# First expert layer of chunks 0 and 1 in seven block products, VectorE's work dealt out by a count for each stretch

## The chip, the core and the metric

One core of one Trainium2 chip runs the whole program. The metric is the device time of one execution in microseconds, the median over several runs.

## What is computed

Attention with a decay (batch 2, 8 heads, 576 positions, head size 64), then a layer of 8 experts whose gates are normalised over rows and columns eight times, then a feed-forward layer with the mish function. All 1152 tokens go through all 8 experts:

```python
x = attention(q, k, v, f)              # 1152 x 512
P = exp(x @ w_gate - max)              # 1152 x 8
for _ in range(8):
    P /= P.sum(1); P /= P.sum(0); P *= N / E
for e in range(8):
    h = maximum(x @ w1[e], 0)          # 512 x 1024: the first expert layer
    out += P[:, e:e+1] * (h @ w2[e])   # 1024 x 512: the second
g = mish(out @ w_in)                   # 512 x 2048
return g @ w_out                       # 2048 x 512
```

## The kernel before

The 1152 tokens are three chunks `c` of 384. An expert is two halves of 512 hidden columns, so there are 16 halves, and a half is four tiles `gg` of 128 columns. A step is one tile of one half for one chunk. Every operand of a matrix product is split into a high and a low part (`xh`, `xl`; `w1h`, `w1l`; `hh`, `hlo`), and a product is made of three: high with high, high with low, low with high.

A step has a first layer (`l1`, L659: 12 matmuls of 128 x 384 into one PSUM tile `ph`), then `relu_split` (L671: ScalarE writes `hh`, VectorE `hlo`), then the second layer of the step before (`l2`, L680: 9 matmuls of 128 x 512 into three accumulators `pa`). So each step's `relu_split` has the second layer of the step before it as cover. After the last tile of an expert VectorE adds the three accumulators, times a column of P, to `acc` (`evict`, L813): nine such additions per expert.

The order is written out by hand (`manual_schedule`): each engine runs its instructions in the order of the code. The attention part ends with half 0 of chunks 0 and 1 (`filler`, L477). Then 184 steps follow (the loop at L855): eight of chunk 2 for expert 0, four each of chunks 0 and 1 for half 1, then 24 for each further expert. Beside them run, handed out one or two to a step: the eight rounds of the normalisation (`sinkhorn`, L693; one round in each of the first steps), the weights' loads and splits (`queue_split`, L779; ScalarE makes the high part, VectorE the low part, GpSimd in its place for half 1), and the decoding of `w_in` and `w_out`, which come as 64-bit numbers (`decode`, L734, and `part`, L758: nine VectorE operations on 128 x 256, 64 times, on every second step). Four weight slots are used in turn. Then come 48 steps of the mish layer (L961). In the attention part, steps `s` below 24 issue `warm(2)`, two small matmuls whose result nobody reads (L590).

## Time and profile before

| | |
|---|---|
| median of 3 runs | 1157.53 us (1154.59 to 1161.88) |
| the profiled execution | 1154.56 us, of which 1152.8 us from the first to the last instruction |
| TensorE (PE) | busy 1137.0 us, 6336 matmuls |
| VectorE (DVE) | busy 726.2 us |
| ScalarE (ACT) | busy 395.7 us |
| GpSimd (POOL) | busy 93.3 us |
| granted TensorE clock | 0.999 of full speed |

The attention part takes the first 180 us, the expert steps run from 180 to 949 us, the mish layer from there to the end. Matmuls overlap, so their own duration is longer than the distance between their starts; that distance is what a matmul costs. A VectorE instruction also starts a little before the end of the one ahead. An idle time is written behind the instruction that ended it, with the instruction that was waited for.

### The profile page before, as it was taken

Reading aid. Unit: us, or ns where it says so; the run is one execution under the profiler, and the core shown is the slowest. Engines: PE = TensorE matmul, PEld = TensorE weight load, DVE = VectorE, ACT = ScalarE, POOL = GpSimd, SP = SyncE. Lnnn points to the kernel's source line nnn. Section 1 sums busy time; section 2 is a strip of 40 time slices with the busy share of each in tenths; the row PEclk is TensorE's granted clock in tenths of the full one; section 3 lists DMA queues with packets and bytes.
Section 4 is the critical chain, followed back from the end, with each engine's and each line's share of the span. In section 5 each row is a group of like instructions: output and inputs, shape, how many; then the busy total and the mean of one; then the engine's idle time right before and its main releaser. Section 6 shows DMA issues by size and latency. Waiting matters only on the chain.

```text
span 1152.8 us, 16871 instructions
## 1 busy us (share of the span) xinstructions
PE 1137.0 (99%) x6336; PEld 1016.4 (88%) x6336; DVE 726.2 (63%) x1755; ACT 395.7 (34%) x864; POOL 93.3 (8%) x127
## 2 busy tenths in 40 slices
PE   8999999999999999999999999999999999999998
PEld 7777778999999999999999999999999999999997
DVE  7966655786657665765675676543222229988887
ACT  6766643322212222221221222122111115555554
POOL 5735423000000000000000000000000000000000
PEclk9999999999999999999999999999999999999999
DMA  6524202343323322331433243221350061000000
GB/s 155 119 62 99 72 13 74 101 130 126 129 73 110 128 92 92 124 127 60 128 116 104 76 144 111 69 69 55 110 183 1 1 220 72 1 29 1 28 1 28
DMA packets 91074, 98.90 MB, mean 86 GB/s; under 512 B 35936, under 2 KB 56160, under 8 KB 90992
## 3 DMA queue, kind: packets, MB, share of 16 engines
q1 hardware_dynamic: 90992, 97.81, 27.5%
q8 instruction: 50, 0.82, 0.3%
q14 instruction: 32, 0.26, 0.1%
HBM read 74.39 MB, written 19.21 MB: 81 GB/s over the span
## 4 chain that ended last, share of the span: by engine, by line
PE 94%; DVE 3%; ACT 1%; issue 1%; POOL 0%; DMA 0%; DVEq 0%; ACTq 0%; POOLq 0%
PE ph L665 42%; PE pa L685 41%; PE x L444 2%; PE pt L420 2%; PE pa L513 1%; PE sp L368 1%; PE ph L494 1%; PE sp L369 1%; PE pt L322 1%; DVE p L381 1%; PE wt L353 1%; PE x L846 0%; DVE rs L399 0%; PE g L460 0%; PE g L465 0%
## 5 line engine op out<-in xcount | busy, mean ns | idle before, releaser
L665 PE MATMUL ph<-xh,w1h 128*128 128x384 f32 x928 | 312.2, 336 | 0.0
L665 PE MATMUL ph<-xh,w1l 128*128 128x384 f32 x928 | 311.8, 336 | 0.0
L665 PE MATMUL ph<-xl,w1h 128*128 128x384 f32 x928 | 311.3, 336 | 0.0
L675 DVE SCALAR_TENSOR_TENSOR hlo<-ph,hh 128x384 fp32r<-128x384 f32 x184 | 102.6, 557 | 304.1 <-ACT hh L674 299.4
L674 ACT ACTIVATE hh<-ph 128x384 fp32r<-128x384 f32 x184 | 90.5, 492 | 575.5 <-PE ph L665 568.3
L685 PE MATMUL pa<-w2h,hh 128*128 128x512 f32 x696 | 273.1, 392 | 0.6 <-ACT hh L940 0.6
L685 PE MATMUL pa<-w2l,hh 128*128 128x512 f32 x696 | 272.6, 392 | 0.0
L685 PE MATMUL pa<-w2h,hlo 128*128 128x512 f32 x696 | 271.7, 390 | 0.0
L665 PEld LDWEIGHTS ph<-xh,w1h 128*128 128x128 f32 x928 | 174.3, 188 | 9.0
L665 PEld LDWEIGHTS ph<-xl,w1h 128*128 128x128 f32 x928 | 174.3, 188 | 8.5
L665 PEld LDWEIGHTS ph<-xh,w1l 128*128 128x128 f32 x928 | 174.3, 188 | 0.0
L685 PEld LDWEIGHTS pa<-w2h,hlo 128*128 128x128 f32 x696 | 130.7, 188 | 28.9 <-DVE hlo L945 0.9
L685 PEld LDWEIGHTS pa<-w2h,hh 128*128 128x128 f32 x696 | 130.8, 188 | 21.2 <-ACT hh L940 1.6
L685 PEld LDWEIGHTS pa<-w2l,hh 128*128 128x128 f32 x696 | 130.8, 188 | 18.9
L391 ACT ACTIVATE p<-p,nmax 128x256 f32<-128x256 f32 (+6 forms) x80 | 48.4, 605 | 13.9 <-DVE nmax L381 11.6
L404 POOL TENSOR_SCALAR p<-p,rs 128x256 f32<-128x256 f32 (+6 forms) x80 | 46.1, 588 | 57.1 <-DVE rs L400 37.7
L827 DVE SCALAR_TENSOR_TENSOR acc<-pa,P,acc 128x512 f32<-128x512 f32 x69 | 47.4, 743 | 0.1
L924 ACT ACTIVATE acc<-acc,two 128x384 f32<-128x384 f32 x48 | 29.6, 617 | 48.6 <-DVE acc L923 48.6
L381 DVE CUSTOM_DVE_ANT_0 p<-sp,mask 128x256 f32<-128x256 f32 (+6 forms) x80 | 37.6, 471 | 6.5 <-PE sp L369 5.3
L94 DVE TENSOR_TENSOR w1l<-stg,w1h 128x512 fp32r<-128x512 f32 x56 | 38.6, 692 | 0.1
L94 DVE TENSOR_TENSOR w2l<-stg,w2h 128x512 fp32r<-128x512 f32 x56 | 38.6, 692 | 0.0
L368 PE MATMUL sp<-kt,qa 128*128 128x256 f32 (+6 forms) x96 | 34.8, 365 | 3.3 <-DVE nmax L381 2.4
(154 smaller groups left out, 1207.6 us busy)
## 6 DMA issues: line engine op xcount, KB each, us to landing
stg<-in_moe_w_dram SPq DMA_DIRECT2D x64, 512.0 KB
raw<-in_moe_w_in_dram SPq DMA_DIRECT2D x32, 256.0 KB
raw<-in_moe_w_out_dram SPq DMA_DIRECT2D x32, 256.0 KB
w_in_h<-db SPq DMA_DIRECT2D x32, 128.0 KB
w_in_l<-da SPq DMA_DIRECT2D x32, 128.0 KB
w_out_h<-db SPq DMA_DIRECT2D x32, 128.0 KB
w_out_l<-da SPq DMA_DIRECT2D x32, 128.0 KB
w1h<-w_in_h SPq DMA_DIRECT2D x4, 1024.0 KB
```

Source lines behind the costliest of these rows:

```text
L94: (lo_engine or nc.vector).tensor_tensor(out=lo, in0=raw, in1=f(hi), op=ALU.subtract)
L368: nc.tensor.matmul(out=t[:n, :w], lhsT=a1, rhs=kt[:, h, ks], start=True, stop=False)
L381: nc.vector.tensor_tensor_reduce(out=p[:n, a, o:o + w], in0=t[:n, :w], in1=mask[:n, m0 + o:m0 + o + w], scale=-1.0, scalar=prev, op0=ALU.a ...
L391: nc.scalar.activation(out=p[:n, a, :nk], in_=p[:n, a, :nk], func=AF.Exp, bias=prev, scale=-1.0, accum_out=u["ssum"][:n, a:a + 1],)
L404: nc.gpsimd.tensor_scalar(out=p[:n, a, :nk], in0=p[:n, a, :nk], scalar1=r[:n, a:a + 1], scalar2=1.0, op0=ALU.mult, op1=ALU.mult,)
L420: nc.tensor.transpose(out=pt[:, o + j * n:o + (j + 1) * n], in_=p[:n, a, j * 128:(j + 1) * 128], identity=idn[:n, :n],)
L665: nc.tensor.matmul(out=ph, lhsT=w[wn][:, kk, fs], rhs=x[c][:, kk], start=(kk == 0 and n == 0), stop=(kk == KD - 1 and n == 2),)
L674: nc.scalar.activation(out=hh, in_=ph, func=AF.Relu)
L675: nc.vector.scalar_tensor_tensor(out=hl, in0=ph, scalar=0.0, in1=f(hh), op0=ALU.max, op1=ALU.subtract)
L685: nc.tensor.matmul(out=pa[j], lhsT=a_[:, ts_], rhs=w[wn][:, ft_, :], start=(first and n == 0), stop=(last and n == 2),)
L827: nc.vector.scalar_tensor_tensor(out=acc[t], in0=pa, scalar=sc, in1=acc[t], op0=ALU.mult, op1=ALU.add)
L924: nc.scalar.activation(out=e_, in_=w_, func=AF.Ln, bias=two)
```

## The change

For halves 1 to 15, the first layer of chunks 0 and 1 is computed together (`pair`). The half's `w1` (512 x 512) and the two chunks (512 x 768) are cut into two by two blocks, and seven products of blocks take the place of eight: four use sums `s` of blocks of `w1`, made anew for each half (`s_sum`, `s_split`), four use sums `t` of blocks of the chunks, made once (`t_whole` on GpSimd, `t_diff` and `t_split`). Each product comes for two row tiles `g`, so a half has 14 products of six matmuls. What products share is kept by adding into the same PSUM bank, and by ScalarE copies of a bank (`take`) that VectorE adds to another bank (`add`). `fin` is the `relu_split` of a finished tile. The lambdas in `plan` stand behind the product that they follow.

The order within a half is now: the 14 products; chunk 2's four first layers; the second layer of chunks 0, 1, 2 one after the other (`second`, 36 matmuls each), with the additions to `acc` after each chunk of each half. So there are 132 such additions for halves 1 to 15. All halves share one weight slot. The splits of the next half's `w1` and the sums lie in `second`, the splits of `w2` in `pair` and behind it. Decoding has seven operations on 128 x 512, with the subtraction that splits the result an eighth, 32 times; `piece(n)` issues the next n of these, at places and in numbers set by the lists `slots`. The tile's buffer is written over with its result, stored, and only then loaded anew.

The eight steps of chunk 2 for expert 0 stay as they were, with all splits and sums of half 1 and the sums `t` beside them. The last two rounds of the normalisation and the nine products with P behind them lie in the first `pair`. The transposes of the mish layer's input are spread otherwise, its weights are loaded in pieces, and `warm(2)` is issued while `s < 32`.

```diff
 class Weights:
...
-    def get(self, half):
-        return self.slots[half % 4]
...
 def attention_moe_kernel(
...
-            if s < 24:
+            if s < 32:
                 warm(2)
...
-        for h2, part in ((1, 0), (1, 2)):
-            wts.load(h2, part)
+        for part in (0, 1):
+            wts.load(1, part, stage)
...
-    for i in (1, 2, 3):
-        wts.add_slot(i, slot_b)
-    ps_a = mctx.enter_context(tc.tile_pool(name="ps_a", bufs=5, space=PSUM))
+    main_w = {n: slot_b.tile([128, 2048], FR, name=f"{n}_1") for n in ("w1h", "w1l", "w2h", "w2l")}
+    sh, sl = (slot_b.tile([128, 2048], FR, name=n) for n in ("sh", "sl"))
+    th, tl = (slot_b.tile([128, 3072], FR, name=n) for n in ("th", "tl"))
+    for half in range(1, 2 * E):
+        wts.slots[half] = {n: pieces(t) for n, t in main_w.items()}
...
+            todo = []
+            if raw64:
+                raw, dst, rs, cs = raw64.pop(0)
+                a_ = dec.tile([128, 512], F32, tag="da", name="da")
+                b_ = dec.tile([128, 512], F32, tag="db", name="db", bufs=1)
...
+                    lambda: v.tensor_scalar(
+                        out=ai, in0=ai, scalar1=0x07FFFFFF, scalar2=3,
+                        op0=ALU.bitwise_and, op1=ALU.logical_shift_left,
+                    ),
+                    lambda: v.scalar_tensor_tensor(
+                        out=ai, in0=hw, scalar=0xC0000000, in1=ai, op0=ALU.bitwise_and, op1=ALU.bitwise_or
+                    ),
...
+            for n, op in enumerate(todo or [None] * 4):
+                if op:
+                    op()
+                if last and n == 0:
+                    nc.scalar.copy(out=hi.bitcast(FR), in_=la)
+                yield
+                if last and n == 2:
+                    v.tensor_tensor(out=lo.bitcast(FR), in0=la, in1=hi, op=ALU.subtract)
+                    for t, d in zip((hi, lo), ldst):
+                        nc.sync.dma_start(out=d[lrs, lcs], in_=t)
+                    yield
+                if last and n == 4:
+                    fetch()
+            parts[0] = (raw, a_, dst, rs, cs) if todo else None
...
+    def piece(n=1):
+        for _ in range(n):
+            next(dec_steps, None)
...
+    def s_sum(half, i):
+        if i == 0:
+            new_sum(half, 0, quad(half, 1, 0), quad(half, 1, 1), ALU.add)
+        elif i == 1:
+            new_sum(half, 1, sums[half, 0], quad(half, 0, 0), ALU.subtract)
+        elif i == 2:
+            new_sum(half, 2, quad(half, 0, 0), quad(half, 1, 0), ALU.subtract)
+        else:
+            new_sum(half, 3, quad(half, 0, 1), sums[half, 1], ALU.subtract)
...
+        t = sums.pop((half, i)).rearrange("p k n -> p (k n)")
+        hi, lo = sh[:, 512 * i:512 * (i + 1)], sl[:, 512 * i:512 * (i + 1)]
+        nc.scalar.copy(out=hi, in_=t)
+        nc.vector.tensor_tensor(out=lo, in0=t, in1=f(hi), op=ALU.subtract)
...
+    def w1_tasks(half, lo_engine=None):
+        def first(i):
+            s_sum(half, i)
+            wts.split(half, i // 2, i % 2, lo_engine)
+            if i == 3:
+                for p in (0, 1):
+                    wts.raw.pop((half, p))
+                if half + 1 < 2 * E:
+                    for p in (0, 1):
+                        wts.load(half + 1, p, stage)
+        f = [lambda i=i: first(i) for i in range(4)]
+        p = [lambda i=i: s_split(half, i) for i in range(4)]
+        return f[:3] + [p[0], f[3]] + p[1:]
...
+    bg = w1_tasks(1)
+    bg = bg[:4] + w2_tasks(1)[:2] + bg[4:6] + w2_tasks(1)[2:] + bg[6:]
...
-    queue_split(1, nc.gpsimd)
+    def t_whole(r, c, k):
+        nc.gpsimd.tensor_tensor(
+            out=r, in0=f(xh[c][:, k:k + 2]), in1=f(xl[c][:, k:k + 2]), op=ALU.add
+        )
...
+    def t_split(i, r):
+        w = 2 * CH
+        r = r.rearrange("p k n -> p (k n)")
+        hi, lo = th[:, w * i:w * (i + 1)], tl[:, w * i:w * (i + 1)]
+        nc.scalar.copy(out=hi, in_=r)
+        nc.vector.tensor_tensor(out=lo, in0=r, in1=f(hi), op=ALU.subtract)
+    tbg = [
+        lambda: (t_whole(r11, 0, 0), t_whole(r12, 1, 0)),
+        lambda: t_whole(r22, 1, 2),
+        lambda: t_diff(r11, r12, r11),
+        lambda: (t_diff(r12, r22, r12), t_split(0, r11)),
+        lambda: (t_diff(r22, r22, r11), t_split(2, r12), t_whole(r11, 0, 2)),
+        lambda: (t_diff(r11, r11, r22), t_split(1, r22)),
+        lambda: t_split(3, r11),
+    ]
...
+    for g in range(NF):
+        half, gg = g // 4, g % 4
+        ph = l1(half, gg, 2, ps_h)
+        h = new_h()
+        relu_split(ph, *h)
+        step_side()
+        for _ in range(2):
+            if bg:
+                bg.pop(0)()
+        if g and tbg:
+            tbg.pop(0)()
...
+    def product(out_, a_, b_, g, first, last):
+        n = 0
+        for kk in range(2):
+            (ah, al), (bh, bl) = a_(kk, g), b_(kk)
+            for u, v_ in ((ah, bh), (ah, bl), (al, bh)):
+                nc.tensor.matmul(
+                    out=out_, lhsT=u, rhs=v_, start=first and n == 0, stop=n == 5, skip_group_check=True
+                )
+                n += 1
...
+    def pair(half, tasks):
+        ops = {
+            1: (a_op(half, 0, 0), b_op(0, 0)), 2: (a_op(half, 0, 1), b_op(1, 0)),
+            3: (s_op(3), b_op(1, 1)), 4: (a_op(half, 1, 1), t_op(3)),
+            5: (s_op(0), t_op(0)), 6: (s_op(1), t_op(1)), 7: (s_op(2), t_op(2)),
+        }
...
+        def new_bank(n, g):
+            bank[n, g] = ps_b.tile([128, 512], F32, tag="b", name="pb")[:, :CH]
+        def take(n, g):
+            t = tmp.tile([128, 512], F32, tag="tmp", name="snap")[:, :CH]
+            nc.scalar.copy(out=t, in_=bank["x", g])
+            snap[n, g] = t
+        def add(n, g, of, with_):
+            t = tmp.tile([128, 512], F32, tag="tmp", name="c")[:, :CH]
+            nc.vector.tensor_tensor(out=t, in0=bank[of, g], in1=snap[with_, g], op=ALU.add)
+            whole[n, g] = t
+        def fin(n, g):
+            src = whole.pop((n, g)) if (n, g) in whole else bank["x", g]
+            i, c = g + (0 if n < 20 else 2), n % 10 - 1
+            relu_split(src, *hpair[i, c])
+        def run(m, g):
+            of = {1: "x", 6: "x", 7: "x", 4: "x", 2: "v", 5: "z", 3: "z"}[m]
+            if m in (1, 2, 5):
+                new_bank(of, g)
+            a_, b_ = ops[m]
+            product(bank[of, g], a_, b_, g, m in (1, 2, 5), m in (4, 2, 3))
+        plan = [
+            (1, 0, [lambda: take("a", 0)]),
+            (2, 0, [lambda: add(11, 0, "v", "a")]),
+            (1, 1, [lambda: take("a", 1), lambda: fin(11, 0)]),
+            (6, 0, [lambda: take("u2", 0)]),
+            (2, 1, [lambda: add(11, 1, "v", "a")]),
+            (5, 0, [lambda: fin(11, 1)]),
+            (7, 0, [lambda: take("u3", 0), lambda: add(22, 0, "z", "u3")]),
+            (6, 1, [lambda: take("u2", 1), lambda: fin(22, 0)]),
+            (5, 1, []),
+            (4, 0, [lambda: fin(21, 0)]),
+            (7, 1, [lambda: take("u3", 1), lambda: add(22, 1, "z", "u3")]),
+            (3, 0, [lambda: add(12, 0, "z", "u2"), lambda: fin(22, 1)]),
+            (4, 1, [lambda: fin(12, 0), lambda: fin(21, 1)]),
+            (3, 1, [lambda: add(12, 1, "z", "u2"), lambda: fin(12, 1)]),
+        ]
+        for k_, (m, g, posts) in enumerate(plan):
+            run(m, g)
+            for p in posts:
+                p()
+            if k_ in tasks:
+                for t in tasks[k_]:
+    def second(half, c, hs, slots, before):
+        pa = [ps_b.tile([128, DM], F32, tag="b", name="pa") for _ in range(3)]
+        for i in range(4):
+            for j in range(3):
+                l2_tile(half, i, pa[j], j, hs[i], i == 0, i == 3)
+            if i == 0:
+                for t in before:
+                    t()
+            for t in slots.pop(0):
+                t()
+        return [lambda j=j: evict(half // 2, c, j, pa[j]) for j in range(3)]
...
-    for idx, (e, c, g, first, last) in enumerate(steps):
-        half, gg = 2 * e + g // 4, g % 4
-        ph = l1(half, gg, c)
-        hh, hl = relu_split(ph)
-        step_side()
-        nbg = 2 if idx < 8 else 1
...
-        if prev:
-            l2(*prev[0])
-            if prev[0][-1]:
-                evict(*prev[1])
...
-        if raw64 and idx >= 10 and idx % 2:
-            decode()
+    for half in range(1, 2 * E):
+        tasks = {}
+        if half > 1:
+            w2t = w2_tasks(half)
+            for t in evicts:
+                t()
+            tasks = {3: [w2t[0]], 5: [w2t[1]]}
+        else:
+            for k_ in (3, 7, 11, 13):
+                tasks[k_] = [step_side]
+        pair(half, tasks)
...
+        h2 = {}
+        if half > 1:
+            for g in range(4):
+                ph = l1(half, g, 2, ps_b, "b")
+                h2[g] = spare[g] if g < 2 else new_h()
+                relu_split(ph, *h2[g])
+                if g in (1, 2):
+                    w2t[g + 1]()
+                    piece(1)
...
+        nxt = w1_tasks(half + 1) if half < last_half else [lambda: None] * 8
+        one_, two_ = lambda: piece(1), lambda: piece(2)
+        if half > 1:
+            slots = [[t, one_] for t in nxt[:4]] + [[]] + [[t, two_] for t in nxt[4:7]] + [[], [nxt[7], two_], [two_], []]
+        else:
+            slots = [[t, one_] for t in nxt[:4]] + [[]] + [[nxt[4], nxt[5]], [nxt[6], one_], [nxt[7], one_]]
...
+        evicts = []
+        for c in range(NCH if half > 1 else 2):
+            hs = [hpair[i, c] for i in range(4)] if c < 2 else h2
+            evicts = second(half, c, hs, slots, evicts)
...
-    tq = [(NCH - 1, kk) for kk in range(KD)]
+    tq = [(c, kk) for c in (1, 2) for kk in range(KD)]
...
-        if 6 <= idx and idx % 2 and tq:
+        if idx >= 4 and tq:
             x2_trans(*tq.pop(0), ps_a, "a")
```

What moves, on VectorE, in the first eight steps. Before, the fifth step held the low part of `relu_split` (hlo), a round of the normalisation, and two splits of weights:

```order
L675 SCALAR_TENSOR_TENSOR hlo_2747<-ph_2733,hh_2746 128x384
L719 TENSOR_SCALAR rc_2752<-cp_2750 128x8
L720 RECIPROCAL rc_2752<-rc_2752 128x8
L721 SCALAR_TENSOR_TENSOR P_94<-P_94,rc_2752 128x72
L709 TENSOR_REDUCE r_2756<-P_94 128x9
L710 TENSOR_SCALAR r_2756<-r_2756 128x9
L711 RECIPROCAL r_2756<-r_2756 128x9
L712 TENSOR_TENSOR P_94<-P_94,r_2756 128x72
L714 TENSOR_REDUCE cs_2761<-P_94 128x8
L94 TENSOR_TENSOR w1l_2_2548<-stg_2677,w1h_2_2547 128x512 x2
```

Now the same step (the fifth) has this; `r` and `tl` are the sums of the chunks' blocks, 768 wide:

```order
L659 SCALAR_TENSOR_TENSOR hlo_2780<-ph_2766,hh_2779 128x384
L705 TENSOR_SCALAR rc_2785<-cp_2783 128x8
L706 RECIPROCAL rc_2785<-rc_2785 128x8
L707 SCALAR_TENSOR_TENSOR P_94<-P_94,rc_2785 128x72
L695 TENSOR_REDUCE r_2789<-P_94 128x9
L696 TENSOR_SCALAR r_2789<-r_2789 128x9
L697 RECIPROCAL r_2789<-r_2789 128x9
L698 TENSOR_TENSOR P_94<-P_94,r_2789 128x72
L700 TENSOR_REDUCE cs_2794<-P_94 128x8
L75 TENSOR_TENSOR w2l_1_2559<-stg_2704,w2h_1_2558 128x512 x2
L911 TENSOR_TENSOR r12_2588<-r22_2589,r12_2588 128x768
L918 TENSOR_TENSOR tl_2563<-r11_2587,th_2562 128x768
```

A sum and a split of 768 columns have been added to the step, and in other steps sums and splits of `w1`.

On VectorE again, in the middle of the expert steps. Before, one step with a decoding in it:

```order
L675 SCALAR_TENSOR_TENSOR hlo_3431<-ph_3417,hh_3430 128x384
L94 TENSOR_TENSOR w1l_0_86<-stg_3288,w1h_0_85 128x512
L742 TENSOR_SCALAR da_3447<-raw64_3383 128x256
L743 TENSOR_SCALAR da_3447<-da_3447 128x256
L744 TENSOR_SCALAR da_3447<-da_3447 128x256
L747 TENSOR_SCALAR db_3448<-raw64_3383 128x256
L748 SCALAR_TENSOR_TENSOR da_3447<-da_3447,db_3448 128x256
L751 TENSOR_SCALAR db_3448<-da_3447 128x256
L752 SCALAR_TENSOR_TENSOR db_3448<-raw64_3383,db_3448 128x256
L753 TENSOR_TENSOR da_3447<-da_3447,db_3448 128x256
L675 SCALAR_TENSOR_TENSOR hlo_3473<-ph_3459,hh_3472 128x384
```

Now the same engine during the 14 products of a half (`c` are the sums `add` makes, `w1h_0` and the like are the buffers of half 0's weights, which now hold `hh` and `hlo`):

```order
L1020 TENSOR_TENSOR c_4062<-pb_4055,snap_4053 128x384
L659 SCALAR_TENSOR_TENSOR w1h_0_85<-c_4062,w1h_0_85 128x384
L75 TENSOR_TENSOR w2l_1_2559<-stg_3840,w2h_1_2558 128x512
L1020 TENSOR_TENSOR c_4092<-pb_4085,snap_4071 128x384
L659 SCALAR_TENSOR_TENSOR w1l_0_86<-c_4092,w1h_0_85 128x384
L75 TENSOR_TENSOR w2l_1_2559<-stg_3840,w2h_1_2558 128x512
L1020 TENSOR_TENSOR c_4115<-pb_4094,snap_4113 128x384
L659 SCALAR_TENSOR_TENSOR w2h_0_87<-c_4115,w2h_0_87 128x384
L659 SCALAR_TENSOR_TENSOR w1l_0_86<-pb_4046,w1l_0_86 128x384
L1020 TENSOR_TENSOR c_4150<-pb_4127,snap_4148 128x384
L1020 TENSOR_TENSOR c_4158<-pb_4094,snap_4081 128x384
```

No decoding stands in the 14 products any more; sums of banks have come in between the low parts.

On TensorE, before, where a first layer ends and the second layer of the step before follows:

```order
L665 MATMUL ph_4453<-xh1_76,w1h_0_85 128x384
L665 MATMUL ph_4453<-xl1_79,w1h_0_85 128x384
L665 MATMUL ph_4453<-xh1_76,w1l_0_86 128x384
L685 MATMUL pa_4450<-w2h_0_87,hh_4428 128x512
L685 MATMUL pa_4450<-w2l_0_88,hh_4428 128x512
L685 MATMUL pa_4450<-w2h_0_87,hlo_4429 128x512
L685 MATMUL pa_4451<-w2h_0_87,hh_4428 128x512
```

Now, where the fourth product follows the third, and adds to the bank of the first (`pb_4046`), which ScalarE has copied out in between:

```order
L996 MATMUL pb_4064<-xh0_75,w1h_1_2556 128x384
L996 MATMUL pb_4064<-xl0_78,w1h_1_2556 128x384
L996 MATMUL pb_4064<-xh0_75,w1l_1_2557 128x384
L996 MATMUL pb_4046<-th_2562,sh_2560 128x384
L996 MATMUL pb_4046<-tl_2563,sh_2560 128x384
L996 MATMUL pb_4046<-th_2562,sl_2561 128x384
```

The second layer has gone from between the first layers; a product of six matmuls follows another.

## Rows read from the trace of the kernel before

**Rows 1.** The page's part 1: engine, busy us, share, instructions.

```profile
PE 1137.0 (99%) x6336; PEld 1016.4 (88%) x6336; DVE 726.2 (63%) x1755; ACT 395.7 (34%) x864; POOL 93.3 (8%) x127
```

**Rows 2.** Timeline of TensorE over one step: start, us, engine, line, operation, out<-in.

```profile
400.60 0.34 PE L665 MATMUL ph<-xh,w1h 128*128 128x384 f32 x1
...
402.68 0.39 PE L685 MATMUL pa<-w2h,hh 128*128 128x512 f32 x1
...
404.73 0.34 PE L665 MATMUL ph<-xh,w1h 128*128 128x384 f32 x1
```

**Rows 3.** Windows: from:to us, PE busy, PEld, DVE, ACT, POOL, clock, DMA share, GB/s.

```profile
50.00:60.00 10.00, 8.42 (x67) 5.87 (x66) 9.02 (x23) 7.39 (x19) 6.91 (x9) 1.00 0.26 60
400.00:600.00 200.00, 200.00 (x1017) 182.36 (x1016) 129.41 (x316) 47.25 (x105) 0.00 (x0) 1.00 0.34 107
1000.00:1100.00 100.00, 100.00 (x509) 91.12 (x508) 87.85 (x174) 54.40 (x102) 0.00 (x0) 1.00 0.04 17
```

**Rows 4.** Groups by line: shapes, count, busy us, mean ns of one, idle before.

```profile
L675 DVE SCALAR_TENSOR_TENSOR hlo<-ph,hh 128x384 fp32r<-128x384 f32 x184 | 102.6, 557 | 304.1 <-ACT hh L674 299.4
L674 ACT ACTIVATE hh<-ph 128x384 fp32r<-128x384 f32 x184 | 90.5, 492 | 575.5 <-PE ph L665 568.3 <-PE mt L698 7.2
L827 DVE SCALAR_TENSOR_TENSOR acc<-pa,P,acc 128x512 f32<-128x512 f32 x69 | 47.4, 743 | 0.1
L94 DVE TENSOR_TENSOR w1l<-stg,w1h 128x512 fp32r<-128x512 f32 x56 | 38.6, 692 | 0.1
L94 POOL TENSOR_TENSOR w1l<-stg,w1h 128x512 fp32r<-128x512 f32 x4 | 5.1, 1304 | 17.6 <-ACT w1h L93 17.6
```

**Rows 5.** Timeline of VectorE in the middle of the expert steps.

```profile
399.77 0.69 DVE L94 TENSOR_TENSOR w1l<-stg,w1h 128x512 fp32r<-128x512 f32 x1
400.38 0.42 DVE L762 TENSOR_TENSOR da<-da,db 128x256 fp32r<-128x256 f32 x1
403.46 0.56 DVE L675 SCALAR_TENSOR_TENSOR hlo<-ph,hh 128x384 fp32r<-128x384 f32 x1 [2.67 <-ACT hh L674]
403.97 0.69 DVE L94 TENSOR_TENSOR w1l<-stg,w1h 128x512 fp32r<-128x512 f32 x1
...
416.27 2.06 DVE L827 SCALAR_TENSOR_TENSOR acc<-pa,P,acc 128x512 f32<-128x512 f32 x3
```

**Rows 6.** Timeline of VectorE in the eighth and ninth steps, and after the last round.

```profile
212.39 0.56 DVE L675 SCALAR_TENSOR_TENSOR hlo<-ph,hh 128x384 fp32r<-128x384 f32 x1 [0.73 <-ACT hh L674]
212.87 0.15 DVE L719 TENSOR_SCALAR rc<-cp 128x8 f32<-128x8 f32 x1
...
214.76 1.28 DVE L94 TENSOR_TENSOR w2l<-stg,w2h 128x512 fp32r<-128x512 f32 x2
216.76 0.56 DVE L675 SCALAR_TENSOR_TENSOR hlo<-ph,hh 128x384 fp32r<-128x384 f32 x1 [0.73 <-ACT hh L674]
...
222.31 3.65 DVE L839 TENSOR_SCALAR acc<-acc,P 128x512 f32<-128x512 f32 x9
```

**Rows 7.** Timeline of all engines in the second step: GpSimd beside VectorE.

```profile
186.85 1.30 POOL L94 TENSOR_TENSOR w2l<-stg,w2h 128x512 fp32r<-128x512 f32 x1 [0.51 <-ACT w2h L93]
...
187.02 1.22 DVE L712 TENSOR_TENSOR P<-P,r 128x72 f32<-128x72 f32 x1
```

**Rows 8.** Timeline of VectorE: the same operation with GpSimd idle.

```profile
214.28 0.23 DVE L712 TENSOR_TENSOR P<-P,r 128x72 f32<-128x72 f32 x1
```

**Rows 9.** Timeline of SyncE: the issue of one 512 KB load.

```profile
412.95 0.38 SPq L70 DMA_DIRECT2D stg<-in_moe_w_dram  x1
```

**Rows 10.** The last half microsecond with its data, a window (columns as in rows 3).

```profile
415.50:416.00 0.50, 0.50 (x4) 0.38 (x3) 0.39 (x2) 0.50 (x2) 0.00 (x0) 1.00 0.55 209
```

**Rows 11.** Timeline of TensorE in the attention part, where `warm` ends.

```profile
45.29 0.61 PE L353 MATMUL wt<-idn 128*128 128x128 f32 x4
45.83 0.94 PE L444 MATMUL x<-pT,v 128*64 128x128 f32 x12
...
52.67 0.50 PE L368 MATMUL sp<-kt,qa 128*128 128x512 f32 x1 [1.55 <-DVE nmax L381]
```

More of the change, by code (lines that the diff above doesn't have):

```diff
@@ L831, in step_side @@
+    started = set()
     def step_side():
@@ L885, in attention_moe_kernel @@
-        if first:
-            psa[e, c] = new_acc()
-        prev = ((half, gg, psa[e, c], hh, hl, first, last), (e, c))
-    assert not (bg or raw64 or decoded)
-    wts.direct(18)
-    free = [a_[:, :CH] for a_ in acc[:6]]
-    scr = {"m": free[:1], "e": free[1:4], "w": free[4:6]}
+            for j in range(3):
+                l2_tile(*prev[:2], psa[j], j, prev[2], prev[3] == 0, prev[3] == NF - 1)
+        prev = (half, gg, h, g)
+    for j in range(3):
+        l2_tile(*prev[:2], psa[j], j, prev[2], prev[3] == 0, prev[3] == NF - 1)
@@ L893, in scratch @@
+    wts.slots[16] = mish_w[16]
+    tp = pieces(th, tl)
+    wts.slots[17] = {"w1h": tp[0:4], "w1l": tp[4:8]}
+    free = [a_[:, :CH] for a_ in acc[:3]]
+    scr = {"m": free[:1], "e": free[1:]}
     def scratch(tag):
```

379 lines of the change are left out of this document (217 added, 162 removed).

## The prediction

> **What bounds the kernel now.** I read the page's first part, then the windows, then a timeline. TensorE is busy for 1137.0 of 1152.8 us, VectorE for 726.2, ScalarE for 395.7 [rows 1]. In the middle of the expert steps TensorE is busy all the time and VectorE for 129.4 of 200 us [rows 3]. Busy time alone proves little, because matmuls overlap; the timeline does more. One step's twelve first-layer matmuls start at 400.60 and its nine second-layer matmuls at 402.68, and the next step at 404.73 [rows 2]. That is 2.08 us or 0.1733 us for a matmul of 384 columns, 2.05 us or 0.228 us for one of 512, and no gap. The other engines wait: ScalarE's `hh` stood idle for 568.3 us until a `ph` was done, VectorE's low part 299.4 us until `hh` was [rows 4]. So in these steps the time is the number of matmuls times these distances, and a matmul less is worth its distance as long as the others keep up in the new order.
>
> **What goes.** In 15 halves, 14 products of six matmuls, 84, stand for the 96 of the first layer of two chunks: 180 matmuls of 384 columns less, times 0.1733: 31.2 us. A half then has 132 such matmuls (22.9 us) and 108 of 512 columns (24.6 us), 47.5 us where twelve steps took 49.6. This is the only gain on the path. VectorE's shorter decoding gains nothing, since TensorE hides VectorE today.
>
> **VectorE in a half.** An operation costs the distance to the next start: 0.61 us for two inputs of 512 columns (399.77 to 400.38), 0.51 for 384 columns (403.46 to 403.97), 0.69 for an addition to `acc` (2.06 for three) [rows 5], 0.41 for one input of 512 columns (3.65 for nine) [rows 6]. The stretches of a half:
>
> - 14 products (14.6 us of TensorE): three additions to `acc` 2.1, six sums and eight low parts 7.1, two splits 1.2: 10.4.
> - Chunk 2's first layers (8.3 us): four low parts 2.0, two splits 1.2, six pieces of decoding 3.1: 6.3. A decoded tile is eight pieces, four with one input and four with two: 4.1 us, 0.51 a piece.
> - The second layers (24.6 us): eight splits and four sums 7.3, six additions 4.1, 14 pieces 7.2: 18.6.
>
> That is 35.3 of 47.5 us; with whole durations (692, 557 and 743 ns [rows 4]) in place of distances it is about 39.5. Both ends leave TensorE the bound, and the six free microseconds of the last stretch lie where VectorE must catch up, before the products. I take no loss.
>
> **Handing over inside the products.** The tightest place: a product that adds to a bank which ScalarE must have copied, with one product, 1.04 us, in between. The matmul that ends a product is done 0.17 us after the next has started (0.34 long, 0.173 apart [rows 2]), the copy of 384 columns takes about the 0.49 us of `hh` [rows 4], together 0.66. It is in time by 0.38. Should another such operation be ahead of it on ScalarE, 0.11 is missing, twice in each of 15 halves: 3 us. I take 0. A sum on VectorE that the last product waits for has two products, 2.08 us, for 0.17 + 0.49 + 0.51 = 1.17.
>
> **The first eight steps.** Here VectorE has a round of the normalisation, 1.89 us (212.87 to 214.76), behind a low part of 0.48, in a step of 4.37 us (212.39 to 216.76) [rows 6]. What comes on top: half 1's splits, which GpSimd had before, its sums, and four differences and four splits of 768 columns, which from 0.51 at 384 and 0.61 at 512 I put at 0.87. By step that makes 3.2, 4.0, 3.6, 5.1, 5.3, 5.3, 4.1, 3.2: 33.8 us in eight steps of 35.0. It fits as a whole; the fourth to sixth overflow by 2.6 us, and about 1.2 of that can lie idle-free behind TensorE, because a step's low part is needed only after the next first layer. Then there are four GpSimd sums of 768 columns, 1.5 times 1.30 = 1.96 us each [rows 4]. Beside a GpSimd sum a small VectorE product took 1.22 us [rows 7] where it takes 0.23 alone [rows 8], 0.99 lost. Four times this is 4.0; three fall into the early steps with room. I take 2 us of waiting for all this, bounds 0 and 33.8 + 7.8 - 35.0 = 6.6, if VectorE stood for the whole of each GpSimd sum.
> The Trainium skill (SBUF — State Buffer, section Who interferes with whom) says that a VectorE instruction with two SBUF inputs and a GpSimd instruction that reads SBUF hold each other off for a whole instruction. The trace agrees: the product ended as the GpSimd sum did. By this rule the sums on GpSimd could cost VectorE up to 7.8 us where the row's loss gives 4.0; the prediction would be at most 4 us higher.
>
> **The first `pair`.** The last two rounds and nine products with P (3.65 us [rows 6]) stand in VectorE's queue ahead of the sum that the last product waits for. The rounds' ends and the nine, 4.4 us, start at about 10 us of the 14.6; the sum then ends near 15.4, and the product could start at 13.7. I take 1.7 us, bounds 0 and 4.4.
>
> **`warm`.** Eight more pairs, 0.54 us each (45.29 to 45.83 [rows 11]): 4.3 us if none is hidden. In that stretch TensorE is busy for 8.42 of 10 us [rows 3], and one wait of 1.55 us for VectorE [rows 11] takes a pair or two. I take 2.2, bounds 0 and 4.3. The granted clock is 1.00 there [rows 3], so there is nothing to win back.
>
> **The mish layer.** The same 36 transposes, eight groups now in consecutive steps, each with a VectorE operation of 0.5. VectorE is busy for 87.85 of 100 us there [rows 3], so a step has about 0.5 free. I take 0.5, bounds 0 and 4.
>
> **Sum.** The profiled execution took 1154.6. 1154.6 - 31.2 + 2.0 + 1.7 + 2.2 + 0.5 = 1129.8. The median of the runs shown is 3.0 us above the profiled execution, the lowest run level with it; I say 1131.
>
> **The rivals.**
> - The front is dearer: first steps, first `pair` and `warm` at their upper ends, 6.6 + 4.4 + 4.3 in place of 5.9, and 3 at the handing over: about 1143. For it: VectorE's overflow in three steps. Against it: the eighth step before already used 3.65 of its 4.37 us on VectorE (0.48 + 1.89 + 1.28 [rows 6]) and still kept its length.
> - A product costs more than its matmuls: each of the 210 opens with a wait of 0.1 us as it turns to another bank: 21 us, 1151. Against it: the second layer changes bank every three matmuls and shows no gap [rows 2]. For it: no row shows a bank added to after another engine has read it.
> - The slower side: VectorE stands waiting for the decoding's data. A tile's buffer is stored before it is loaded anew, and the next tile starts two pieces later. A load of 512 KB took 3.05 us from issue (412.95 [rows 9]) to its last data (416.0 [rows 10]); the two stores are about the same again, 6 us for a turn, 2.5 turns a half. If nothing covers them, VectorE needs 35.3 + 15 = 50.3 us for a half, and 2.8 us more than 47.5 in each of 13 halves is 36 us: 1167. It decides from 12.2 us of waiting per half on. Against it: three pieces and up to three sums and splits, 2.5 to 5 us, lie between store and load, and a turn that falls on the products costs nothing. I expect under 5 us a half.
> - The losses hide: 1122 to 1124.
>
> **How the numbers follow.** Forecast 0.54 (alone 1124 to 1138), dearer front 0.16, dearer products 0.16, decoding 0.09, no losses 0.05. A measurement of this kernel can tell about 1% from no change, here below 1146 or above 1169. The forecast, the dearer front, the case without losses and a quarter of the dearer products are faster: 0.79; the rest of these are the same: 0.12; slower 0.09. The range leaves out the decoding's case and the upper part of the dearer products, 0.15: 1122 to 1150.
>
> **What would show it.** Right: a half repeats every 47.5 us; 0.173 us between the starts of a product's matmuls across a change of bank; TensorE's idle time before `pb` rows near nothing from half 2 on; a few us of it in the first eight steps, by VectorE or `cp`, and before the last product of the first `pair`. Wrong: idle time before `pb` rows in every half, by ScalarE's `snap` or VectorE's `c` (handing over), or a VectorE that waits for `raw` and comes late to the additions of chunk 2; a first stretch that ends over 10 us late.

## The result, and the profile of the changed kernel

The changed kernel takes 1140.99 us in the median (1139.93 to 1141.42, four executions), the kernel before on the same chip 1159.7 (1154.59 to 1161.88): a ratio of 0.9843, 95% interval 0.9806 to 0.9881, so 1.6% faster. 1131 was forecast, with 1122 to 1150 as range. The direction and the mechanism hold, the size does not: the two profiled executions differ by 13.1 us (1154.56 and 1141.42) where the sum has 24.8.

The page's part 1 of the changed kernel; TensorE is still the busiest engine by far, with 148 matmuls fewer than in [rows 1] (180 in the products, against 32 more records of filling ones), and VectorE and ScalarE have more to do:

```profile
PE 1121.1 (98%) x6188; PEld 993.2 (87%) x6188; DVE 831.2 (73%) x1724; ACT 472.7 (41%) x986; POOL 91.0 (8%) x123
```

One half from TensorE's timeline (start, us, engine, line, operation, out<-in; some rows, cuts marked by dots): 108 second-layer matmuls from 567.64, 84 of the products from 592.74, 48 of chunk 2's first layer from 607.34, and the next half at 615.66:

```profile
567.64 0.39 PE L674 MATMUL pa<-w2h,w1h 128*128 128x512 f32 x1
...
592.74 0.34 PE L996 MATMUL pb<-xh,w1h 128*128 128x384 f32 x1
...
607.34 0.34 PE L651 MATMUL ph<-xh,w1h 128*128 128x384 f32 x1
...
615.66 0.39 PE L674 MATMUL pa<-w2h,w1h 128*128 128x512 f32 x1
```

The half is 48.02 us. Products: 14.60 / 84 = 0.1738 us a matmul; chunk 2: 8.32 / 48 = 0.1733; both as forecast. The second layers: 25.10 / 108 = 0.2324 us, where [rows 2] gave 0.228. Of these, the 90 that read the outputs in their new places take 0.2332 (567.64 to 588.63), the last 18, which read the small tiles `hh` and `hlo`, 0.2283. The same three stretches as windows (columns as in [rows 3]):

```profile
567.64:592.74 25.10, 25.10 (x109) 20.31 (x109) 21.12 (x38) 6.09 (x11) 0.00 (x0) 1.00 0.46 147
592.74:607.34 14.60, 14.60 (x86) 14.60 (x85) 8.26 (x16) 7.09 (x15) 0.00 (x0) 1.00 0.18 56
607.34:615.66 8.32, 8.32 (x49) 8.32 (x49) 5.97 (x12) 3.01 (x6) 0.00 (x0) 1.00 0.08 32
```

TensorE is busy throughout and the clock is 1.00; nothing waits, and yet the stretch is 0.5 us too long. TensorE's waits from 180 us to the end (what waited, for what: total us, times, longest), the four largest ones:

```profile
PE cp L703 <- DVE cs L700: 1.4, 1, 1.4
PE pb L996 <- DVE c L1020: 1.4, 1, 1.4
PE pb L996 <- DVE acc L805: 1.1, 1, 1.1
PE ph L651 <- DVE acc L810: 0.8, 1, 0.8
```

Each occurs once, none in the repeated halves.

Where the missing 11.6 us are (1141.4 against the sum's 1129.8):

| stretch | sum | measured, and how | more |
|---|---|---|---|
| second layers of 15 halves | 0.228 each | half 48.02 in place of 47.5, 14 times; in half 1 16.8 (239.81 to 256.60) in place of 16.4 | +7.7 |
| first 28 score matmuls | 0 | 54.77 against 53.01, below | +1.8 |
| `warm` | 2.2 | 70.43 against 66.43, less 1.76 | 0.0 |
| first eight steps | 2.0 | 184.24 to 222.99 is 38.75; before 35.95 | +0.8 |
| first `pair` | 1.7 | one wait of 1.4 | -0.3 |
| mish layer | 0.5 | wait 0.8; then 196.9 us to the last nine matmuls against 194.4, less four groups of transposes more at 0.37 | +1.4 |

That is 11.4 of 11.6. Three rows of the attention part, the 24th, the 28th and the 34th score matmul with `kb`, of the changed kernel and then of the kernel before:

```profile
46.89 0.34 PE L351 MATMUL sp<-kb,qb 96*128 96x384 f32 x1
...
54.77 0.39 PE L351 MATMUL sp<-kb,qb 96*128 96x512 f32 x1
...
70.43 0.30 PE L351 MATMUL sp<-kb,qb 96*64 96x288 f32 x1
```

```profile
45.12 0.34 PE L369 MATMUL sp<-kb,qb 96*128 96x384 f32 x1
...
53.01 0.39 PE L369 MATMUL sp<-kb,qb 96*128 96x512 f32 x1
...
66.43 0.30 PE L369 MATMUL sp<-kb,qb 96*64 96x288 f32 x1
```

The 1.76 us at the start are not the change's: they stand at the 24th score matmul already (46.89 against 45.12), ahead of the first filling matmul that the change adds (49.65). TensorE came to its first keys 0.37 us later in that execution, after a wait of 1.74 us where the kernel before has 1.36, and behind this wait the granted clock was partly at its lower level, 1.2 GHz. Three of the eight added pairs stand between the 24th and the 28th, and this stretch takes 7.88 us with them and 7.89 without: they are hidden. The other five cost the 2.24. The windows of 10 to 20 us (TensorE's busy time, clock, DMA share, GB/s), changed kernel and kernel before:

```profile
10.00:20.00 10.00, 8.37 (x52) 0.66 0.53 107
```

```profile
10.00:20.00 10.00, 7.50 (x67) 1.00 0.58 120
```

Of the four executions of the changed kernel one had a mean clock of 1.000; it took 1139.93 us.

### The profile page after: what moved, and what is told of

The parts are those of the page before. It is cut to its first block, busy times and chain, and to the rows that moved or that the text cites. A ratio compares the mean times of both kernels' runs of the same rounds, so it can differ in the third digit from the quotient of the medians.

```text
span 1139.6 us, 16413 instructions
## 1 busy us (share of the span) xinstructions
PE 1121.1 (98%) x6188; PEld 993.2 (87%) x6188; DVE 831.2 (73%) x1724; ACT 472.7 (41%) x986; POOL 91.0 (8%) x123
## 4 chain that ended last, share of the span: by engine, by line
PE 92%; DVE 5%; POOL 1%; ACT 1%; issue 1%; DVEq 0%; POOLq 0%; ACTq 0%
PE pa L674 41%; PE ph L651 20%; PE pb L996 19%; PE x L426 2%; PE pt L402 2%; PE pa L495 1%; PE sp L350 1%; PE ph L476 1%; PE wt L335 1%; PE pt L304 1%; PE sp L351 1%; DVE p L363 1%; POOL kb L181 1%; PE x L831 0%; DVE rs L381 0%
## 5 line engine op out<-in xcount | busy, mean ns | idle before, releaser
L651 PE MATMUL ph<-xh,w1h 128*128 128x384 f32 x352 | 118.6, 337 | 0.8 <-DVE acc L810 0.8
L651 PE MATMUL ph<-xh,w1l 128*128 128x384 f32 x304 | 102.4, 337 | 0.1
L651 PE MATMUL ph<-xl,w1h 128*128 128x384 f32 x304 | 102.2, 336 | 0.0
L674 PE MATMUL pa<-w2h,w2h 128*128 128x512 f32 x225 | 77.2, 396 | 0.0
L674 PE MATMUL pa<-w2h,w1l 128*128 128x512 f32 x225 | 76.8, 396 | 0.0
L674 PE MATMUL pa<-w2h,w1h 128*128 128x512 f32 x225 | 76.8, 396 | 0.0
L674 PE MATMUL pa<-w2h,hh 128*128 128x512 f32 x180 | 71.1, 395 | 0.0
L651 PEld LDWEIGHTS ph<-xh,w1h 128*128 128x128 f32 x352 | 66.2, 188 | 2.0 <-DVE acc L810 1.3
L651 PEld LDWEIGHTS ph<-xl,w1h 128*128 128x128 f32 x304 | 57.2, 188 | 0.6
L651 PEld LDWEIGHTS ph<-xh,w1l 128*128 128x128 f32 x304 | 57.2, 188 | 0.4 <-DVE w1l L75 0.4
```

The costliest lines, as they stand in the source:

```text
L651: nc.tensor.matmul(out=ph, lhsT=w[wn][kk][:, fs], rhs=x[c][:, kk], start=(kk == 0 and n == 0), stop=(kk == KD - 1 and n == 2),)
L674: nc.tensor.matmul(out=pa, lhsT=a_[:, ts_], rhs=w[wn][ft_], start=(first and n == 0), stop=(last and n == 2),)
```

## Experiments on the products and the filling matmuls

**The products undone.** In place of the fourteen products and what follows them, eight plain passes:

```diff
-        for k_, (m, g, posts) in enumerate(plan):
-            run(m, g)
-            for p in posts:
-                p()
+        for k_ in range(14):
+            if k_ in (0, 2, 4, 5, 7, 9, 11, 13):
+                i, c = divmod((0, 2, 4, 5, 7, 9, 11, 13).index(k_), 2)
+                relu_split(l1(half, i, c, ps_b, "b"), *hpair[i, c])
```

> The changed kernel with the seven block products of each half replaced by the eight plain passes of the kernel before (12 matmuls each), in the new place and order and with the stored halves; the sums and splits are still made and go unread, the snapshots and additions from PSUM fall away. Theory: 12 matmuls more of 0.1733 us in each of 15 halves are 31.2 us more, less 1.4 us that the first pair waited: a half of 50.1 us and about 1170 us, so that the new arrangement without its products would be some 0.5 to 1.3 per cent slower than the kernel before (its 49.6 us half), by slower 512-column matmuls, the front and the filling matmuls. Rival: the products lose part of their saving in hand-overs of banks, snapshots and additions, and the plain passes cost clearly less than 25 us more.

1169.99 us (1169.95 to 1170.09), 1.0095 of the kernel before (1.0058 to 1.0132). A half's second layers, the products' place, and the next half, from its timeline:

```profile
582.00 0.39 PE L674 MATMUL pa<-w2h,w1h 128*128 128x512 f32 x1
```

```profile
607.11 0.34 PE L651 MATMUL ph<-xh,w1h 128*128 128x384 f32 x1
```

```profile
632.07 0.39 PE L674 MATMUL pa<-w2h,w1h 128*128 128x512 f32 x1
```

50.07 us, 2.05 more than 48.02 for 12 matmuls, 0.171 each; the whole is 29.0 us slower, 29.8 were expected. So the products save all that the 12 matmuls are worth (2.08), and the rival with a price for each product falls. It also shows the other side: the new arrangement alone is slower than the old one, and its second layers take 25.11 us here too, without any product.

**`warm` to 24 steps again**, in the changed kernel (`if s < 32:` to `if s < 24:`), and **to 32 steps alone**, in the kernel before (`if s < 24:` to `if s < 32:`).

> The changed kernel with the count of the filling matmuls in the attention part put back to 24 steps. Theory: the 16 added filling matmuls lie on TensorE's path at 0.14 us each, so the first matmul of the expert part comes 2.2 us earlier than in the changed kernel, and the time is 1138 to 1139 us. Rival: they fill time in which TensorE would wait anyway, and nothing changes; or without them the granted clock of a stretch up to 60 us drops below 1.00, and the part becomes longer than before.

> The kernel before with one part of the change alone: the filling matmuls run for 32 steps of the attention part in place of 24. Theory A: they cost their 16 x 0.14 = 2.2 us on TensorE's path and also keep the granted clock up; the executions of the kernel before lie in two groups (about 1155 us at a mean clock of 0.998 to 1.000, about 1160.5 us at 0.993 to 0.994), and with the filling only one group stays, near 1157 us, so that the median falls by some 3 us although the profiled execution gets 2.2 us longer. Theory B: the two groups have another cause, both move up by 2.2 us, and the median rises to about 1162 us.

The first: 1138.34 to 1144.75 us, median 1141.05, where the changed kernel stays within 1139.93 to 1141.42. In its profiled execution 50 to 60 us is the window that shows both sides, TensorE as little busy as in [rows 3], and the clock partly at 1.2 GHz (columns as in the windows above):

```profile
50.00:60.00 10.00, 8.43 (x56) 0.83 0.17 40
```

The second: ten executions between 1156.87 and 1158.29, none near 1160, while the kernel before beside it spread over 1155.03 to 1161.79, those at a mean clock of 0.993 or 0.994 at 1159.8 and above. The ratio of the medians is 0.9999 (0.9984 to 1.0014). So the filling matmuls cost about 2 us where the clock would have stayed up (at a mean clock of 1.000: 1155.03 without them, 1156.87 and 1157.03 with them; in the changed kernel 1138.34 and 1139.93), and save 2 to 4 us where it would not. Over all runs, 42 executions with 32 steps show no mean clock below 0.996; of the kernel before, nine of the 34 beside the experiments lie at 0.993 or 0.994. No trace shows in which stretch of those nine the clock was lower. In this set the median hardly moves; the spread does. Theory A is right about the executions at the lower clock and wrong about the median.

## Experiments on the second layers

**64 bytes further.** A matmul reads two operands from SBUF: the stationary one (`lhsT` in the code) and the moving one (`rhs`). In a second layer the first-layer output is stationary and the weights move. In the built program the tiles in which the changed kernel keeps its first-layer outputs (the four of `first_w`) begin 64 bytes past a multiple of 256, the small `hh` and `hlo` tiles and the weights of the halves at one.

```diff
-    hs_ = [t[:, CH * i:CH * (i + 1)] ...
+    hs_ = [t[:, 16 + CH * i:16 + CH * (i + 1)] ...
```

> The changed kernel with one number different: the stored outputs of the first layer begin 64 bytes further into their tiles, so that they start at a multiple of 128 bytes (the tiles themselves start 64 bytes past one; the two small tiles that the kernel before used start at one). Theory A, placement: the 512-column matmuls that read them as stationary operand stand 0.2325 us apart because of where they lie, and fall to the 0.228 us of those that read the small tiles; a half repeats every 47.6 us in place of 48.02 and the time falls by about 6 us to about 1134 us. Theory B, neighbours: the 0.2325 comes from the work of VectorE and ScalarE beside the matmuls, or from so many of them in a row; distance, half and time stay (0.2325, 48.0, 1140 to 1141 us).

1140.57 us, half 48.04. Theory A as it was worded, a multiple of 128, falls.

**Less decoding beside them.** Five of the seven operations of a decoding piece are left out.

```diff
+            todo = todo[:2] + [lambda: None] * (len(todo) - 2)
```

> The changed kernel with five of the seven VectorE operations of every decoding piece left out (the decoded weights are therefore not those of the reference; loads, casts, splits and stores stay). VectorE has about 2.6 us less to do for a piece, some 6.5 us in a half. Theory A, placement: the distance of the 512-column matmuls stays 0.2325 us, the half 48.0 us, and the time 1140 us. Theory B, neighbours: with fewer VectorE operations beside them the distance falls towards 0.228 and the half towards 47.5. A third, that VectorE's decoding or its wait for raw data holds TensorE somewhere in the halves: TensorE's waits there fall and with them the half; the waits in the trace give it less than 0.1 us a half.

One time, 1141.13 us, half 48.02. VectorE has 15.88 us of work in the second layers in place of 21.12, and they take the same 25.10:

```profile
567.35:592.45 25.10, 25.10 (x109) 20.30 (x109) 15.88 (x27) 6.09 (x11) 0.00 (x0) 1.00 0.47 146
```

Theory B, as far as it means VectorE's work, falls: a quarter less of it, and the distance is the same to the last digit. So does the third: decoding holds nothing up.

**Places exchanged.** The first two outputs of chunk 0 go to the small tiles (`near[i] = new_h()` in `fin`), the last two of chunk 2 to where those were (`hpair[g - 2, 0]` in place of `new_h()`).

> The changed kernel with four stored outputs in each other's places: the first two of chunk 0 go into the small tiles that two of chunk 2 had, and those two of chunk 2 where chunk 0's were. Theory A, placement: the quick matmuls (0.228 us apart) move from the end of the 108 of a half to their beginning, the first 18 taking 4.1 us in place of 4.2; half and time stay at 48.0 and 1140 us. Theory C, position: the matmuls at the end of the row stay the quick ones, because of where they stand in the row and not of what they read.

1139.77 us (one time), half 48.00. The first second-layer matmul and the first that reads another tile, from the timeline:

```profile
566.22 0.39 PE L674 MATMUL pa<-w2h,hh 128*128 128x512 f32 x1
...
570.31 0.40 PE L674 MATMUL pa<-w2h,w1l 128*128 128x512 f32 x1
```

18 matmuls in 4.09 us, 0.227 each, now at the beginning; the ones at the end take 0.233. What they read decides, not where they stand in the row.

**The matmul by itself.** Behind the last output, stretches of 36 matmuls without a reader, each built like this:

```diff
+        for i in range(4):
+            for j in range(3):
+                js = slice(j * 128, (j + 1) * 128)
+                for n, (s_, m_) in enumerate(((sth(i), mh(i)), (sth(i), ml(i)), (stl(i), mh(i)))):
+                    nc.tensor.matmul(
+                        out=pas[j][:, :cols], lhsT=s_[:, js], rhs=m_[:, :cols],
...
```

> The changed kernel, and behind its last output fourteen stretches of 36 matmuls each, twice, that nobody reads: the same form of second-layer matmul with the stationary operand and the moving operand taken from one place of SBUF or another, while no other engine works. Theory A, placement: the stretch that reads the stored outputs where the changed kernel keeps them (prb, with the second-layer weights of the halves as moving operand) shows 0.2325 us from matmul to matmul, the one that reads the small tiles of the kernel before (pra) 0.228 us. Theory B, neighbours: with nothing beside them both show 0.228 us. The other stretches (first-layer weights, the sums, the products' operands, the tokens as stationary operand; 384 columns; 64 bytes further) show which places cost, if any.

The first matmul of some stretches in the second pass, and the last of all:

```profile
1246.19 0.40 PE L1271 MATMUL pra<-w2h,hh 128*128 128x512 f32 x1
...
1254.39 0.40 PE L1271 MATMUL prb<-w2h,w1h 128*128 128x512 f32 x1
...
1262.78 0.40 PE L1271 MATMUL prc<-w2h,hh 128*128 128x512 f32 x1
...
1271.04 0.39 PE L1271 MATMUL prd<-w2h,w1h 128*128 128x512 f32 x1
...
1279.20 0.39 PE L1271 MATMUL pre<-w2h,th 128*128 128x512 f32 x1
...
1333.00 0.39 PE L1271 MATMUL prl<-w2h,w1h 128*128 128x512 f32 x1
...
1341.18 0.40 PE L1271 MATMUL prm<-w2h,w1h 128*128 128x512 f32 x1
...
1349.55 0.39 PE L1271 MATMUL prn<-w2h,w1h 128*128 128x512 f32 x1
...
1357.71 0.40 PE L1271 MATMUL prn<-w2h,w1l 128*128 128x512 f32 x1
```

A distance is the difference of two starts over 36 (35 for the last). With the bytes by which each operand begins past a multiple of 256:

| stretch | stationary | moving | us a matmul |
|---|---|---|---|
| `pra` small tiles; `pre`, `prf`, `pri`, `prl` others | 0 | 0 | 0.2267 to 0.2278 |
| `prd` | 64 | 64 | 0.2267 |
| `prc` | 0 | 64 | 0.2294 |
| `prb`, `prg`, `prh`, `prn` | 64 | 0 | 0.2331 to 0.2333 |
| `prm` | 128 | 0 | 0.2325 |

Placement it is, with no other engine at work; and not the region alone, since `prd` reads its stationary operand from the same tiles as `prb` and `prm` and is quick. Of the places tried, equal ones within 256 bytes are quick, unequal ones are not. At 384 columns the two stretches (64 and 64, 0 and 64) both show 0.1733. It explains the 64 bytes too: they led from 64 to 128.

**192 bytes further.** `48 + CH * i` in place of `CH * i` puts the stored outputs at a multiple of 256.

> The changed kernel with the stored outputs of the first layer 192 bytes further into their tiles, so that they begin at a multiple of 256 bytes, as the second-layer weights do that are the moving operand beside them. Theory A, both operands must begin at the same place within 256 bytes: all 512-column matmuls of the halves come to 0.227 to 0.228 us, a half to 47.5 us, and the time falls by 14 x 0.5 + 0.4, about 7 to 8 us, to 1133 us. Theory B, it is the region of SBUF that counts and not the place within 256 bytes: 0.2325 us, 48.0 us and 1140 us stay.

1132.79 us (1132.24 to 1133.33), 0.9785 of the kernel before (0.9756 to 0.9814). Its half:

```profile
563.26 0.39 PE L674 MATMUL pa<-w2h,w1h 128*128 128x512 f32 x1
...
587.76 0.34 PE L996 MATMUL pb<-xh,w1h 128*128 128x384 f32 x1
...
602.35 0.34 PE L651 MATMUL ph<-xh,w1h 128*128 128x384 f32 x1
...
610.67 0.39 PE L674 MATMUL pa<-w2h,w1h 128*128 128x512 f32 x1
```

24.50 / 108 = 0.2269 us, and 47.41 us a half, 0.1 below the forecast's 47.5. With the same tiles and only the start moved, the region as a cause falls too. One number in the code gives back 8 us.

One half of this run is longer, 48.08 us. In it a product waits for a ScalarE copy that stands behind a high part on ScalarE, the case that the prediction named under the handing over and put at 0; the high part, from 450.69 us on, had itself waited 1.97 us for a sum on VectorE:

```profile
451.63 0.44 PE L996 MATMUL pb<-th,sh 128*128 128x384 f32 x1 [0.34 <-ACT snap L1015]
```

It comes once in fourteen repeats, and not at all in the changed kernel.

## Experiments on the front, and both together

**Another order on VectorE.**

```diff
+    for j in range(3):
+        evict(0, 2, j, psa[j])
     for t in bg + tbg:
         t()
-    for j in range(3):
-        evict(0, 2, j, psa[j])
...
-            for k_ in (3, 7, 11, 13):
+            for k_ in (3, 13):
                 tasks[k_] = [step_side]
```

> The changed kernel with two of VectorE's pieces in another order: the evictions of the first chunk-2 result stand ahead of the last sums and splits, and the last normalisation round with the nine scalings (3.65 us) is run behind the last product of the first pair, not in its middle. Theory: TensorE's wait for the eviction (1.05 us) and its wait for the addition in the first pair (1.4 us) go, and 2.0 to 2.5 us are gained, about 1138.5 us; its wait of 1.4 us for the column sums stays. Rival: VectorE is as late elsewhere, the waits turn up at the next product or second layer, and less than 0.5 us is gained.

1138.34 us (1138.17 to 1139.26). Half of the theory holds: the wait in the first `pair` is gone; the others stand:

```profile
PE cp L703 <- DVE cs L700: 1.4, 1, 1.4
PE pb L996 <- DVE acc L805: 1.0, 1, 1.0
```

From the first product to the second layers it is 15.05 us (222.54 to 237.59) in place of 16.82; at a mean clock of 1.000 the two kernels took 1138.17 and 1139.93 us. The first half of the edit moved nothing: its list is empty by then, and the last split still stands ahead of the eviction in VectorE's queue. VectorE's timeline of this kernel:

```profile
220.84 0.95 DVE L918 TENSOR_TENSOR tl<-r,th 128x768 fp32r<-128x768 f32 x1
221.71 0.69 DVE L805 COPY acc<-pa 128x512 f32<-128x512 f32 x1
```

The product starts at 222.54, when the copy is done. An eviction ahead of that split was not tried.

**Without GpSimd's last sum** (`t_whole(r11, 0, 2)` taken out).

> The changed kernel without the last of the four sums that GpSimd makes in the first eight steps (one operand of products 4 and 6 is therefore wrong). Theory: that sum, 2.46 us on GpSimd, lies beside a VectorE multiplication of 72 columns that takes 1.02 us in place of its usual 0.23 us; without it this multiplication takes 0.23 us, the column sums come 0.8 us earlier, TensorE's wait for them falls from 1.4 to about 0.6 us, and the time by 0.8 us. Rival: VectorE is late there by its own work, the multiplication stays long or the wait stays near 1.4 us.

In the changed kernel GpSimd's sum and VectorE's multiplication, from two timelines:

```profile
213.43 2.46 POOL L906 TENSOR_TENSOR r<-xh,xl 128x768 f32<-128x768 f32 x1 [28.92 <-DVE r L911]
```

```profile
214.96 1.02 DVE L707 SCALAR_TENSOR_TENSOR P<-P,rc 128x72 f32<-128x72 f32 x1
```

Without the sum, the multiplication and TensorE's wait:

```profile
214.43 0.23 DVE L707 SCALAR_TENSOR_TENSOR P<-P,rc 128x72 f32<-128x72 f32 x1
```

```profile
PE cp L703 <- DVE cs L700: 0.6, 1, 0.6
```

The multiplication loses 0.79 us, and the wait falls by 0.8; the first product starts 37.98 us after the first expert matmul in place of 38.75. The multiplication ends as the sum does, as in [rows 7]. The Trainium skill (SBUF — State Buffer, section Who interferes with whom) has a VectorE instruction with two SBUF inputs and a GpSimd instruction that reads SBUF contend, under a lock that is exclusive; the trace agrees, the multiplication of 1.02 us ended 0.09 us after the sum. The other three sums cost nothing because they had run before: GpSimd took them one behind another as the attention part ended, and was done at 184.51, with the first of the eight steps starting at 184.24:

```profile
178.98 5.53 POOL L906 TENSOR_TENSOR r<-xh,xl 128x768 f32<-128x768 f32 x3 [7.60 <-issue]
```

The single time, 1140.04 us, is too coarse for 0.8.

**The shift and the order together.**

> The shift of 192 bytes and the other order of VectorE's pieces in the first pair together. If both act as they do alone: 1133 us less the 2.2 us of the other order, 1130.5 to 1131.5 us. If the one takes the other's gain: 1132.5 us or more.

1130.83 us (1129.59 to 1131.6), 0.977 of the kernel before (0.9736 to 0.9805): 2.3% faster, and 0.9% below the changed kernel. In the same set the shift alone has 1132.79, so the order adds 2.0 to it: the two gains add.

**All operands at a multiple of 256 by padding**, in place of the shift (48 elements ahead of `xh`, 16 ahead of `acc`).

> The kernel of the shift and the other order, with the places made equal by two pieces of padding (192 and 64 bytes) in place of the shift: the tokens, both sets of weights, the sums and the stored outputs all begin at a multiple of 256 bytes; only the two big tiles of the attention part stay 32 bytes past one. Theory A, the same place within 256 bytes is what counts: the halves stay at 47.4 us, and the first-layer matmuls of the last layer's third and fourth quarter, whose weights lay in both places by turns (0.1755 us apart against 0.1736 in the other quarters), come to 0.1736 as well, 0.5 to 1 us less in all, about 1130 us. Theory B, that the shift of 192 bytes acted through something else: the halves go back to 48.0 us and the time to 1138 us.

1131.81 us (1131.06 to 1132.0). The halves stay at 47.43 us, as theory A has it; one of them is 48.55, again by a wait for a ScalarE copy (0.80). The theory's second half falls. One step of the last layer, first layer, second layer and the next step, with padding and then with the shift (the kernel of the run before):

```profile
1051.08 0.33 PE L653 MATMUL ph<-xh,w1h 128*128 128x384 f32 x1
...
1053.19 0.63 PE L676 MATMUL pa<-more,hh 128*128 128x512 f32 x2
...
1055.27 0.33 PE L653 MATMUL ph<-xh,w1h 128*128 128x384 f32 x1
```

```profile
1049.66 0.34 PE L651 MATMUL ph<-xh,w1h 128*128 128x384 f32 x1
...
1051.74 0.62 PE L674 MATMUL pa<-more,hh 128*128 128x512 f32 x2
...
1053.79 0.34 PE L651 MATMUL ph<-xh,w1h 128*128 128x384 f32 x1
```

The nine second-layer matmuls take 2.08 us (0.2311 each) where the shift has 2.05, and so in every step behind the transposes; the twelve first-layer ones take 2.10 to 2.11 in all of these steps, where the shift has 2.08 in about half. All operands begin at equal places there, so equal places are not enough in that layer, where VectorE is busy for 85.94 of the 100 us from 1000 us on. What counts there stays open.

## Why the prediction was right in kind and too large in size

- **What goes.** Right: 180 matmuls at 0.1733 are worth 31.2 us, and the plain passes show it from the other side. The step that failed is the other term of the same sum, "108 of 512 columns (24.6 us)". The distance 0.228 was read from matmuls that read the small tiles, and taken over for outputs that the change stores elsewhere. The 90 matmuls of a half that read those take 0.2332 us, with the other 18 a mean of 0.2324: 25.1 us a half, 7.7 us in all. With the outputs at the weights' place it is 0.2269. I had bounds for waits and for a product, none for a matmul that only reads from another place.
- **VectorE in a half.** 35.3 us forecast, 35.35 measured (21.12 + 8.26 + 5.97). The stretches were off, 18.6 for the second layers and 10.4 for the products, but there was room. No loss, as said.
- **Handing over inside the products.** None: not one wait for a copy or an addition from half 2 on. The margin is small, though: with halves of 47.41 us one product waited.
- **The first eight steps.** 2.8 us, 2.0 forecast, within the bounds. Of its parts the loss beside a GpSimd sum is right in kind (0.79 a time, 0.99 forecast) but came once: the forecast had three of the four sums in early steps with room, and they ran before these steps altogether. Of the rest, 0.6 us is the part of the wait for the column sums that stays without the sum; the other 1.05 us, the first product behind the eviction behind the last split, are VectorE's overflow in another place than I had looked for it, at the end and not in the fourth to sixth step.
- **The first `pair`.** 1.4 us, 1.7 forecast, for the reason given: the other order takes it away.
- **`warm`.** 2.2 us, as forecast, in the profiled execution, with three of the eight pairs hidden where I had a pair or two. "There is nothing to win back" was wrong: it was drawn from one execution at a clock of 1.00, and others of the same kernel were not.
- **The mish layer.** 1.9 us in place of 0.5: one wait of 0.8 for an eviction, and steps 1.1 us longer in all, part of them by first layers of 2.10 to 2.11 us, not 2.08, in some of its steps, which the padding didn't mend. The cause is open.
- **The rivals.** Dearer products: fell, by the plain passes. The dearer front: its 1143 is near the time, but it is not what happened: the front cost 6.4 us, not 15.3. The decoding's data: VectorE's idle time before `da`, for the raw data, is 52.8 us in twelve halves, 4.4 a half, under the 5 that I allowed, and behind TensorE. The losses hide: no.
- **The range.** 1141 lies in 1122 to 1150, but by luck as to the cause: the room was left for a dearer front and dearer products, and neither came. The place of an operand was not among the rivals.
- The profiled execution of the kernel before is one of its quickest. Against the median the gain looks larger, 18.7 us, because two of the four executions in that set took 1161.88; in the sets beside the experiments the kernel before has medians from 1156.34 to 1160.51.

## What to carry to other kernels

A distance between matmuls taken from a trace holds for the operands that it was read from; when a change stores an operand elsewhere, look where it begins against the other operand, and try a shift of the start before anything larger. A stretch in which an engine is busy all the time, waits for nothing and is still too long wants its instruction measured by itself, alone on the chip. And a kernel whose executions differ in their granted clock wants them all looked at: what costs 2 us in one profile can save as much or more in the next execution.

## What the runs showed of the hardware that I had not expected

- Second-layer matmuls (fp32r, 512 columns moving) stand 0.2267 to 0.2278 us apart when both operands begin at the same place within 256 bytes, and 0.2294 to 0.2333 when they do not, with no other engine at work; the halves of the kernel show the same, 0.2269 and 0.2332. In this kernel that is 8 us. Matmuls of 384 columns show no difference, and in the last layer, beside a VectorE busy for 86%, equal places gave 0.2311.
- The granted clock of 10 to 20 us varies from one execution to the next, with means of 0.66, 0.83 and 1.00, in kernels whose code is the same there (the changed kernel 0.66, with the shift and the other order 1.00). What decides it the runs don't show.
